# Attention folded into a feed-forward layer: products of one head each, grouped by parity and packed eight to the array, with decode clamps on GpSimd and a new early order

## The chip, the cores and the metric

The kernel runs on one core of a Trainium2 chip (trn2). The metric is the device time of one launch in microseconds (us). Before the change three runs gave 717.12, 719.28 and 719.66 us; the median is 719.28. All data start and end in the chip's main memory (DRAM). A core has five engines with their own instruction streams: TensorE (PE), VectorE (DVE), ScalarE (ACT), GpSimd (POOL) and SyncE (SP); nearly all transfers are issued by SP.

## The reference, cut to what matters

```python
B, H, S, Ns, D = 8, 8, 512, 32, 64           # x [B,H,S,D], state [B,H,Ns,D]
scores  = x @ state.T / sqrt(D)              # per batch and head, 512 x 32
xread   = softmax(scores) @ state            # 512 x 64
scores2 = state @ x.T / sqrt(D)              # the transpose of the same scores
sread   = softmax(scores2) @ x               # 32 x 64
t = concatenate([xread, sread])              # 544 tokens a batch, 8 heads x 64 = 512 features
out = (maximum(t @ w_in, 0) ** 2) @ w_out    # w_in 512 x 2048, w_out 2048 x 512
```

There are 8 x 544 = 4352 tokens. Inputs x and state are float32; w_in and w_out arrive as 64-bit floats, which the kernel reads as pairs of 32-bit words and turns into float32 on the chip ("decode").

## The kernel before, in words

**The fold.** xread @ w_in is softmax(scores) @ (state @ w_in), head by head. So the kernel never forms xread. It makes, for each batch b, the matrix W2[b] = state_h @ w_in_h for the eight heads h: 8 x 32 = 256 rows and 2048 columns. The first layer for the 512 x-tokens of a batch is then a product over K = 256 (two groups of 128 rows, called g) of the softmax and W2[b]. The 256 sread tokens of all batches are "block 8" and use w_in itself (K = 512).

**The two large steps.** The 2048 hidden columns are 16 pieces `fc` of 128, two to an `hb` of 256. Wide products are exact to about float32: each operand is split into a high part and a remainder (`_hi`, `_lo`, type float32r) and three products are added (`mm3`, line 325): hi x hi, hi x lo, lo x hi. `hidden(blk, fc)` makes 128 x 512 hidden values in PSUM (tile `ph`, 6 matmuls of 512 columns), ACT and DVE square them and split them into `g_hi` and `g_lo`. `accumulate(blk, fc)` adds their products with w_out into four PSUM tiles `acc` (12 matmuls of 512 columns). Blocks 0 and 1 are done in two halves of eight `fc`; their partial results wait in DRAM.

**W2 before** has three ways. `direct_w2` (batches 0 and 1) multiplies in float32: `by_head` (line 349) uses the array in parts of 64 rows and 32 columns, with heads 4g..4g+3 at the four column strips and the row half given by the head's parity; one call of `direct_w2` makes 8 such matmuls, 256 columns each. `quad_w2` (lines 705 and 706; tile `qps`, batches 2 to 5) stacks four batches' states of a head to 128 rows and uses whole-array float32r products. `paired_w2` (tile `w2ps`, from `mm3`, batches 6 and 7) uses block-diagonal states and three products. Results of all but hb 0 to 3 of batches 0 and 1 go to DRAM and come back through `load_w2`.

**Scores before.** For batches 0 and 1 `scores` calls `by_head` in float32, 4 matmuls for each g. For the others x is transposed by DVE, split (lines 302 and 303) and multiplied by block-diagonal states `bd_hi` and `bd_lo` (tile `st`, 6 matmuls of 512 columns for each g). `sread` (line 515, tile `pr`) makes 16 small matmuls for each g. `transposes` (line 500) prepares it. `prep` makes the transposed x.

**Decode.** A piece of 128 x 512 weights takes one operation on ACT (line 337, absolute value) and four on DVE: a clamp (338), a shift (339) and two that merge bits (340, 341). There are 16 pieces of w_in (`decode_wi`) and 16 of w_out (`prep_wo`).

**What sets the order.** PLAN is a long string of steps ("hidden.2.4 accumulate.2.2 ..."); they are walked in that order, and a step's needs must stand ahead of it. SECOND is a table that sends single operations to the second of two engines. On top of that the framework's scheduler, which simulates a timeline, may move instructions past one another on each engine; instructions marked `keep_in_program_order` stay. PSUM has eight banks in three pools: four for `acc`, two for `ph`, two for everything else (`ps_b`, tag `psb`: W2, scores of batches 1 to 7, transposes, sread). SBUF buffers are shared by tags, so a tile waits until the last user of its buffer is done.

Of the kernel before, what the change touches and what calls it, by code (L numbers as in the profile page):

```python
# [18 lines left out]

# [4 lines left out]

PLAN = """
    load_raw.0 load_wo.1 zero_bd.1.1 load_direct ident neg_ident decode_wi.0 load_raw.1 decode_wi.1 start.0
        prep.0.0 load.0.1 prep.0.1 zero_bd.0.1 load_raw.3 start.1 load_raw.2 load_wo.4 states scores.0.0
        direct_w2.0 decode_wi.3 decode_wi.2 load_wo.0 direct_w2.1 load_wo.2 transposed_scores.0.0 exp_s.0.0
        transposes.0.0 softmax.0.0 sread.0.0 prep_wo.0 load_wo.3 direct_w2.2 load_wo.7 scores.0.1
        transposed_scores.0.1 exp_s.0.1 prep_wo.1 transposes.0.1 prep.1.0 sread.0.1 prep_wo.3 scores.1.0  # L30
        transposed_scores.1.0 load_raw.5 load_raw.4 load.1.1 direct_w2.3 softmax.0.1
    hidden.0.0 accumulate.0.0 prep.1.1 prep_wo.2
    hidden.0.1 decode_wi.4 decode_wi.5 load_wo.5 direct_w2.4 scores.1.1 load_raw.6 decode_wi.6 prep_wo.4
        load_raw.7
    hidden.0.2 direct_w2.6 exp_s.1.0 direct_w2.5 transposed_scores.1.1
# [11 lines left out]
    hidden.1.4 decode_wi.14 qw2.0.13 accumulate.1.2 decode_wi.15 accumulate.1.4 qw2.0.14
    hidden.1.1 accumulate.1.1
    hidden.1.5 accumulate.1.5
    hidden.0.8  # L50
    hidden.1.6 prep_wo.13 accumulate.1.3 qw2.0.15 load_wo.14 load_quad.1 prep_wo.14 load_w2.0.5 accumulate.1.6
    hidden.1.7 load_wo.15
    hidden.0.9 load_w2.0.7 start.2 prep.2.0 sread.1.1 load_w2.0.6 qload.1.4 scores.2.0 prep_wo.15
        accumulate.0.8 prep_quad.1 qload.1.0 qprep.1.0 qprep.1.4 accumulate.0.9
    hidden.0.10
# [21 lines left out]
    hidden.2.5 load_w2.2.3 scores.3.0 qw2.1.10
    hidden.2.4 qload.1.13 qw2.1.11 qprep.1.13 accumulate.2.2
    hidden.2.6 load_w2.2.4 accumulate.2.1 qload.1.14 load_w2.2.5 load.3.1 prep.3.1 qprep.1.12 qw2.1.12
    hidden.2.7 qw2.1.13 accumulate.2.4 accumulate.2.6  # L80
    hidden.2.8 qprep.1.14 qload.1.15 qprep.1.15 load_w2.3.0 qw2.1.14 accumulate.2.7 transposed_scores.3.0
        load_n.3.0
    hidden.2.10 exp_s.3.0
    hidden.2.9 transposes.3.0 load_w2.2.6
    hidden.2.12 scores.3.1 accumulate.2.3 transposed_scores.3.1 qw2.1.15 load_w2.2.7 load_quad.2
        accumulate.2.8 sread.3.0 accumulate.2.10 softmax.3.0 softmax.3.1
    hidden.2.11 split_wi.0 split_wi.1 accumulate.2.9 load_w2.3.1
# [129 lines left out]
def tile_attn_moe(  # L217
# [791 lines left out]
```

## Time and profile before

| what | value |
|---|---|
| runs | 717.12, 719.28, 719.66 us; median 719.28 |
| span of the profiled execution | 715.2 us, which is 4.1 below the median of the runs |
| PE, DVE, ACT, POOL busy | 676.1, 409.6, 377.1, 118.4 us |
| instructions counted | PE 3797, DVE 734, ACT 725, POOL 118 |
| moved by DMA | 113.57 MB, mean 159 GB/s |

The profile is of one execution. A row of a group gives a line of the kernel, the engine, the operation, "output<-inputs" with tile names without their numbers, the shape, a count, the busy time, the mean time of one, and the idle time of the engine just ahead of these instructions with what ended it. A row of the timeline gives the start, the length and the same names. A float32 product in parts of the array appears as two records, so x16 in such a row is eight matmuls of the program. Matmuls overlap: the length of one is a latency, and its price is the distance to the start of the next.

### The profile page before, as it was taken

To read this page: it belongs to the slowest core of one execution; us is meant where nothing else is said; L and a number is where in the kernel's file an instruction comes from. 1 tells how busy PE (TensorE), PEld (TensorE's weight loads), DVE (VectorE), ACT (ScalarE), POOL (GpSimd) and SP (SyncE) were. 2 spreads that over 40 slices of the span, in tenths; PEclk is the share of its full clock that TensorE was granted. 3 is DMA by queue.
4 is the path that set the end of the run, shared out by engine and by line. 5 is a ranking of instruction groups with operands and counts; after the bars stand their busy time and mean duration, and the time that the engine had idled before them with its cause. 6 is when DMAs were issued, how large, how long until landed. Compare 5 with 4: busy or idle time off the path is not lost.

```text
span 715.2 us, 10699 instructions
## 1 busy us (share of the span) xinstructions
PE 676.1 (95%) x3797; PEld 542.4 (76%) x3797; DVE 409.6 (57%) x734; ACT 377.1 (53%) x725; POOL 118.4 (17%) x118
## 2 busy tenths in 40 slices
PE   4497889999999999999999999999999999999997
PEld 2265566677888788888878888888888888888886
DVE  4999889599665587574444564466347222322233
ACT  3576664577665466555535565556455443333323
POOL 1321222044101214123220230012011000000000
PEclk9699999999999999999999999999999999999999
DMA  9936576645764753664426244752576334444402
GB/s 240 261 95 216 176 250 194 233 148 175 238 196 136 203 177 107 207 216 151 147 76 212 98 148 134 248 165 87 163 206 185 81 83 131 127 118 119 118 1 88
DMA packets 93797, 113.57 MB, mean 159 GB/s; under 512 B 24752, under 2 KB 63920, under 8 KB 93744
## 3 DMA queue, kind: packets, MB, share of 16 engines
q1 hardware_dynamic: 93600, 112.76, 51.5%
q8 instruction: 30, 0.49, 0.3%
q14 instruction: 23, 0.19, 0.1%
q10 hardware_dynamic: 144, 0.13, 0.1%
HBM read 70.39 MB, written 42.47 MB: 158 GB/s over the span
## 4 chain that ended last, share of the span: by engine, by line
PE 79%; DVE 7%; issue 4%; DMA 4%; ACT 2%; SPq 1%; POOL 1%; DVEq 0%; ACTq 0%; POOLq 0%
PE acc L325 45%; PE ph L325 25%; PE st L325 2%; PE w2ps L325 2%; PE pr L515 1%; DMA xp<-in_x_dram 1%; DMA part_d<-po 1%; PE w2ps L349 1%; PE qps L705 1%; PE qps L706 1%; PE pt L500 1%; DVE deco L341 1%; DVE g_lo L766 1%; DVE deco L340 1%; DMA std<-in_state_dram 1%
## 5 line engine op out<-in xcount | busy, mean ns | idle before, releaser
L325 PE MATMUL acc<-wo,g_hi 128*128 128x512 f32 x1086 | 312.9, 392 | 4.4 <-ACT g_hi L761 4.3
L325 PEld LDWEIGHTS acc<-wo,g_hi 128*128 128x128 f32 x1086 | 200.8, 188 | 49.0 <-ACT g_hi L761 6.4
L325 PE MATMUL acc<-wo,g_lo 128*128 128x512 f32 x543 | 187.4, 393 | 1.0 <-ACT g_lo L764 0.5
L325 PE MATMUL ph<-k_hi,w 128*128 128x512 f32 x512 | 182.9, 399 | 3.5 <-DVE g_lo L766 3.1
L766 DVE TENSOR_TENSOR g_lo<-ph,g_hi 128x512 fp32r<-128x512 f32 (+1 forms) x139 | 90.6, 654 | 119.7 <-ACT g_hi L761 115.4
L325 PEld LDWEIGHTS acc<-wo,g_lo 128*128 128x128 f32 x543 | 100.6, 188 | 22.6 <-DVE g_lo L766 1.5
L325 PEld LDWEIGHTS ph<-k_hi,w 128*128 128x128 f32 x512 | 97.2, 191 | 26.5 <-DVE g_lo L766 4.2
L761 ACT CAST g_hi<-ph 128x512 fp32r<-128x512 f32 (+1 forms) x144 | 81.0, 564 | 50.3 <-DVE ph L760 35.3
L325 PE MATMUL ph<-k_lo,w 128*128 128x512 f32 x256 | 101.1, 395 | 0.1
L760 DVE SCALAR_TENSOR_TENSOR ph<-ph,r 128x512 f32<-128x512 f32 (+1 forms) x78 | 51.1, 655 | 70.5 <-ACT r L759 70.4
L759 ACT ACTIVATE r<-ph 128x512 f32<-128x512 f32 (+1 forms) x78 | 44.3, 568 | 83.0 <-PE ph L325 82.9
L755 ACT ACTIVATE ph<-ph 128x512 f32<-128x512 f32 (+1 forms) x66 | 37.2, 566 | 66.6 <-PE ph L325 66.3
L325 PEld LDWEIGHTS ph<-k_lo,w 128*128 128x128 f32 x256 | 48.7, 190 | 9.8 <-POOL k_lo L303 0.9
L303 POOL TENSOR_TENSOR w<-w_f,w 128x512 fp32r<-128x512 f32 x19 | 25.2, 1324 | 120.0 <-ACT w L302 111.3
L756 ACT ACTIVATE ph<-ph 128x512 f32<-128x512 f32 (+1 forms) x66 | 37.7, 571 | 1.2
L349 PE MATMUL w2ps<-dec,sT 64*32 64x256 f32 x256 | 18.4, 412 | 18.3 <-DVE dec L341 10.6
L302 ACT CAST w<-w_f 128x512 fp32r<-128x512 f32 x40 | 24.7, 616 | 17.1 <-DMA w_f<-w_d 11.9
L391 DVE STREAM_TRANSPOSE xT<-xp 128x512 f32<-128x512 f32 x24 | 16.9, 706 | 24.1 <-DMA xp<-in_x_dram 22.4
L349 PEld LDWEIGHTS w2ps<-dec,sT 64*32 64x32 f32 x256 | 7.4, 112 | 26.0 <-issue 11.4
L303 POOL TENSOR_TENSOR x_lo<-xT,x_hi 128x512 fp32r<-128x512 f32 x10 | 13.3, 1328 | 80.9 <-ACT x_hi L302 58.4
L325 PE MATMUL ph<-sr_hi,s 128*128 128x256 f32 x128 | 25.5, 282 | 0.0
L302 ACT CAST x_hi<-xT 128x512 fp32r<-128x512 f32 x24 | 14.9, 620 | 14.2 <-DVE xT L391 12.4
(124 smaller groups left out, 783.0 us busy)
## 6 DMA issues: line engine op xcount, KB each, us to landing
wi_raw<-in_moe_w_in_dram SPq DMA_DIRECT2D x16, 512.0 KB, 4.4
wo_raw<-in_moe_w_out_dram SPq DMA_DIRECT2D x16, 512.0 KB, 5.4
w_d<-qo SPq DMA_DIRECT2D x64, 128.0 KB, 2.1
w_f<-w_d SPq DMA_DIRECT2D x32, 256.0 KB, 3.4
win_d<-wi SPq DMA_DIRECT2D x16, 512.0 KB, 3.2
w<-w2a_d SPq DMA_DIRECT2D x32, 256.0 KB, 4.1
s<-win_d SPq DMA_DIRECT2D x128, 64.0 KB, 2.0
out_dram<-o SPq DMA_DIRECT2D x31, 256.0 KB, 3.8
```

Of the source, the lines that this page charges most:

```text
L302: nc.scalar.copy(hi, src)
L303: pick(key, nc.gpsimd, nc.vector).tensor_sub(lo, src, hi.bitcast(F32))
L325: m = nc.tensor.matmul(ps, l, r, start=first and i == 0, stop=last and i == len(seq) - 1, skip_group_check=skip)
L340: nc.vector.scalar_tensor_tensor(v, high, 0xC0000000, v, ALU.bitwise_and, ALU.bitwise_or)
L349: nc.tensor.matmul(out[v], sT[0][q, NC * b + 2 * g + h // 2], x[q], start=start, stop=stop, tile_position=(64 * (h % 2), 32 * h), **kw,)
L391: nc.vector.transpose(xT.rearrange("p (k j s) -> p k j s", k=KC, j=4), self.xp[g].rearrange("p (j k d) -> p k j d", j=4, k=KC)[..., 32 * e ...
L755: nc.scalar.activation(ph, ph, AF.Relu)
L756: nc.scalar.activation(ph, ph, AF.Square)
L759: nc.scalar.activation(r, ph, AF.Relu)
L760: nc.vector.scalar_tensor_tensor(ph, ph, 0.0, r, ALU.max, ALU.mult)
L761: nc.scalar.copy(ghi, ph)
L766: nc.vector.tensor_sub(glo, ph, ghi.bitcast(F32))
```

## The change: what it does

- **Heads by parity.** `by_head` now makes eight products of 64 rows and 32 columns: head 2c + g at column strip c and row half g. The two halves write to two different PSUM banks (`out[g]`). The states of all batches lie in `sT` in this layout; `load_states` and `states` fill it for batches 0 and 1 and then for 2 to 7. Block-diagonal states, `prep_state`, `zero_bd` and the split of x are gone.
- **Scores** of all batches, both groups at once, are one call of `by_head` in float32 (8 matmuls of 512 columns).
- **W2** of all batches is made by `two_w2`, for two batches and one hb at a time: 16 matmuls of 256 columns into two `psb` tiles, that is, both buffers of that pool. There are 8 hb x 4 pairs = 32 such calls, from `direct_w2` (0 and 1), `later_w2` (2 and 3, 4 and 5) and `last_w2` (6 and 7). `quad_*`, `paired_*` and `split_wi` are gone. Float32 w_in is read back from DRAM by `load_wf`.
- **sread** is one step for both groups (32 matmuls into one PSUM tile).
- **Decode**: the clamp is on POOL for 13 of the 16 pieces of w_in (all but 0, 2 and 3) and for 14 of w_out (all but 5 and 10), 27 of 32 in all.
- **Loads**: x of batches 2 to 7 comes in 8 transfers for each g instead of 4; the weights of block 8 come as float32 and are split on the chip (`load_wi`), where before their two parts were read back.
- **Order**: PLAN's early part does `direct_w2` for hb 0 and 1, scores and softmax of batch 0, sread of batch 0 and one piece of w_out ahead of the first hidden step; steps of batch 1 and more pieces of w_out, which stood there before, come behind it. From there on accumulate follows hidden at a distance of two steps almost throughout.

```diff
-    def by_head(out, b, g, h, x, start, stop, **kw):
-        q, v = slice(64 * (h % 2), 64 * (h % 2) + 64), slice(32 * h, 32 * h + 32)
-        nc.tensor.matmul(
-            out[v], sT[0][q, NC * b + 2 * g + h // 2], x[q],
-            start=start, stop=stop, tile_position=(64 * (h % 2), 32 * h), **kw,
-        )
+    def by_head(out, b, x, start, stop, **kw):
+        for c in range(NC):
+            for g in range(G):
+                q, v = slice(64 * g, 64 * g + 64), slice(32 * c, 32 * c + 32)
+                nc.tensor.matmul(
+                    out[g][v], sT[q, NC * b + c], x(c)[q],
+                    start=start, stop=stop, tile_position=(64 * g, 32 * c), **kw,
+                )
...
+    def two_w2(hb, b0, last):
+        w = (wf.pop(hb) if last else wf[hb]).bitcast(F32)
+        ps = [ps_b.tile([P, 2, HB], F32, tag="psb", name=f"w2ps{hb}_{b0}_{g}") for g in range(G)]
+        for b in range(2):
+            by_head([t[:, b] for t in ps], b0 + b, lambda c: w[:, c], b == 0, True, skip_group_check=True)
+        return ps
...
+    def keep_w2(hb, b0, ps):
+        for g in range(G):
+            o = p2.tile([P, 2, HB], F32, tag="o", name=f"w2o{hb}_{b0}_{g}", bufs=4)
+            evac(f"w2_out.{hb}.{b0}.{g}", o, ps[g])
+            nc.sync.dma_start(w2_d[hb][b0 : b0 + 2, :, g].rearrange("b p f -> p b f"), o)
+
+    def later_w2(hb, b0):
+        keep_w2(hb, b0, two_w2(hb, b0, b0 == 4))
...
-                mm3(
-                    st,
-                    [((bhi[:, g * E + e], blo[:, g * E + e]), (x[0][:, e], x[1][:, e])) for e in range(E)],
-                )
+            for g in range(G):
+                self.st[g] = pool.tile([P, S], F32, tag=tag, name=f"st{b}_{g}")
+            by_head(self.st, b, lambda c: self.x[c // 2][:, c % 2], True, True)
...
-        nc.vector.tensor_scalar(vf, vf, F64_HI_MIN, F64_HI_MAX, ALU.max, ALU.min)
+        eng = pick(key, nc.vector, nc.gpsimd)
+        eng.tensor_scalar(vf, vf, F64_HI_MIN, F64_HI_MAX, ALU.max, ALU.min)
...
-                nc.tensor.matmul(ps[:, h2], s4[0][:, h], t[:, c, h2], start=True, stop=False)
-                nc.tensor.matmul(ps[:, h2], s4[1][:, h], t[:, c, h2], start=False, stop=True)
...
-            mm3(ps[:, c], [((s4[0][:, k], s4[1][:, k]), (w[:, c, 0], w[:, c, 1]))])
...
-                        nc.sync.dma_start(t[32 * h : 32 * h + 32, 2 * i : 2 * i + 2].bitcast(F32), rows[:, :, j])
+            split(hi[:, q], lo[:, q], f[:, q], f"w_in_lo.{hb}.{i}")
...
-    hidden.4.8 scores.5.1 qw2.2.6 load_w2.4.6 accumulate.4.6 transposed_scores.5.1
+    hidden.4.8 softmax.5.0 load_n.5.0 load_n.5.1 accumulate.4.6
```

**Where the order changes: PE, W2 of batches 2 to 5.** Before, in the stretch of hidden block 0, `fc` 12, the eight matmuls of one `quad_w2` call stand as one piece between accumulate and hidden (`qps` is the PSUM tile, `tt` the split weights, `s_hi` and `s_lo` the split states):

```order
L325 MATMUL acc_8_3_1476<-wo_985,g_lo_10_1529 128x512
L705 MATMUL qps_0_0_1616<-tt_1499,s_hi 128x256
L706 MATMUL qps_0_0_1616<-tt_1499,s_lo 128x256
L705 MATMUL qps_0_1_1625<-tt_1499,s_hi 128x256
L706 MATMUL qps_0_1_1625<-tt_1499,s_lo 128x256
L705 MATMUL qps_0_0_1616<-tt_1499,s_hi 128x256
L706 MATMUL qps_0_0_1616<-tt_1499,s_lo 128x256
L705 MATMUL qps_0_1_1625<-tt_1499,s_hi 128x256
L706 MATMUL qps_0_1_1625<-tt_1499,s_lo 128x256
L325 MATMUL ph_12_1658<-k_hi_149,w_0_6_1450 128x512
```

Now, at the same place of the program, eight matmuls of the pair 2 and 3 and eight of the pair 4 and 5 stand in the middle of an accumulate (a tile `w2ps_2_1` belongs to the pair that begins with batch 2, row half 1):

```order
L291 MATMUL acc_8_0_2085<-wo_1212,g_hi_10_1992 128x512 x2
L291 MATMUL acc_8_0_2085<-wo_1212,g_lo_10_1993 128x512
L291 MATMUL acc_8_1_2086<-wo_1212,g_hi_10_1992 128x512 x2
L317 MATMUL w2ps_2_1_2038<-wf_1_1841,sT 32x256 x8
L317 MATMUL w2ps_4_0_2061<-wf_1_1841,sT 32x256 x8
L291 MATMUL acc_8_1_2086<-wo_1212,g_lo_10_1993 128x512
L291 MATMUL acc_8_2_2087<-wo_1212,g_hi_10_1992 128x512 x2
```

The whole-array products of `quad_w2` are gone, and the products in parts of the array stand with all eight of one row half in a row.

**PE, W2 of batches 6 and 7.** Before, one `paired_w2` call stands as one piece between hidden block 3, `fc` 9, and accumulate:

```order
L325 MATMUL ph_9_3451<-k_hi_2262,w_3_4_3195 128x512
L325 MATMUL w2ps_2_3598<-wi_3342,s_hi 128x256 x2
L325 MATMUL w2ps_2_3598<-wi_3342,s_lo 128x256
L325 MATMUL w2ps_2_3598<-wi_3342,s_hi 128x256 x2
L325 MATMUL w2ps_2_3598<-wi_3342,s_lo 128x256
L325 MATMUL acc_0_0_3049<-wo_760,g_hi_6_3386 128x512 x2
```

Now the first call of `last_w2`, in block 2 and 3, stands like this, with eight more of its matmuls some 25 rows further on:

```order
L291 MATMUL acc_0_3_2508<-wo_1639,g_lo_15_3049 128x512
L317 MATMUL w2ps_6_0_3238<-wf_2_2863,sT 32x256
L317 MATMUL w2ps_6_1_3239<-wf_2_2863,sT 32x256
L291 MATMUL ph_2_3152<-k_hi_2308,w_3_1_3055 128x512
L291 MATMUL ph_2_3152<-k_lo_2309,w_3_1_3055 128x512
L291 MATMUL ph_2_3152<-k_hi_2308,w_3_1_3055 128x512 x2
L291 MATMUL ph_2_3152<-k_lo_2309,w_3_1_3055 128x512
L291 MATMUL ph_2_3152<-k_hi_2308,w_3_1_3055 128x512
L317 MATMUL w2ps_6_0_3238<-wf_2_2863,sT 32x256
L317 MATMUL w2ps_6_1_3239<-wf_2_2863,sT 32x256
L317 MATMUL w2ps_6_0_3238<-wf_2_2863,sT 32x256
L317 MATMUL w2ps_6_1_3239<-wf_2_2863,sT 32x256
```

The 16 matmuls of one call are spread over several places between hidden and accumulate.

**DVE, the first operations.** Before, both clamps (L338) of the first two pieces of w_in stand on DVE (`sT` is the transpose of the states):

```order
L338 TENSOR_SCALAR dec_133<-dec_133 128x512
L339 TENSOR_SCALAR dec_133<-dec_133 128x512
L340 SCALAR_TENSOR_TENSOR dec_133<-wi_raw_117,dec_133 128x512
L541 STREAM_TRANSPOSE sT<-std_122 128x256
L341 SCALAR_TENSOR_TENSOR dec_133<-wi_raw_117,dec_133 128x512
L338 TENSOR_SCALAR dec_142<-dec_142 128x512
L339 TENSOR_SCALAR dec_142<-dec_142 128x512
L340 SCALAR_TENSOR_TENSOR dec_142<-wi_raw_140,dec_142 128x512
```

Now the second piece has no clamp there; it is the L305 of POOL:

```order
L305 TENSOR_SCALAR wf_128<-wf_128 128x512
L478 STREAM_TRANSPOSE sT<-std_103 128x256
L306 TENSOR_SCALAR wf_128<-wf_128 128x512
L307 SCALAR_TENSOR_TENSOR wf_128<-wi_raw_101,wf_128 128x512
L308 SCALAR_TENSOR_TENSOR wf_128<-wi_raw_101,wf_128 128x512
L306 TENSOR_SCALAR wf_128<-wf_128 128x512
L307 SCALAR_TENSOR_TENSOR wf_128<-wi_raw_114,wf_128 128x512
L308 SCALAR_TENSOR_TENSOR wf_128<-wi_raw_114,wf_128 128x512
```

The clamp of the second piece has moved from DVE to POOL, and the transposed states have moved up by two places.

More of the change, by code (lines that the diff above doesn't have):

```diff
@@ L47 @@
[L47 to L55, printed above, removed]
@@ L77 @@
[L77 to L86, printed above, removed]
@@ new lines @@
+    hidden.2.12 accumulate.2.10
+    hidden.2.13 sread.3 load_w2.3.0 accumulate.2.11
+    hidden.2.14 accumulate.2.12
+    hidden.2.15 load_w2.3.1 accumulate.2.13
+    hidden.3.0 start.4 accumulate.2.14
+    hidden.3.1 load_w2.3.2 accumulate.2.15
+    hidden.3.2 load.4.1 prep.4.0 accumulate.3.0
+    hidden.3.3 load_w2.3.3 accumulate.3.1
+    hidden.3.4 last_w2.2 load_wf.2.3 accumulate.3.2
+    hidden.3.5 prep.4.1 load_w2.3.4 accumulate.3.3
+    hidden.3.6 accumulate.3.4
+    hidden.3.7 scores.4 transposed_scores.4.0 exp_s.4.0 transposed_scores.4.1 exp_s.4.1 load_w2.3.5
+        accumulate.3.5
@@ new lines @@
+    hidden.3.8 softmax.4.0 load_n.4.0 load_n.4.1 accumulate.3.6
+    hidden.3.9 load_w2.3.6 accumulate.3.7
+    hidden.3.10 softmax.4.1 last_w2.3 load_wf.2.4 accumulate.3.8
+    hidden.3.11 transposes.4.0 transposes.4.1 load_w2.3.7 accumulate.3.9
+    hidden.3.12 accumulate.3.10
+    hidden.3.13 sread.4 load_w2.4.0 accumulate.3.11
+    hidden.3.14 accumulate.3.12
+    hidden.3.15 load_w2.4.1 accumulate.3.13
+    hidden.4.0 start.5 accumulate.3.14
+    hidden.4.1 load_w2.4.2 accumulate.3.15
+    hidden.4.2 load.5.1 prep.5.0 accumulate.4.0
@@ new lines @@
+    hidden.4.12 accumulate.4.10
+    hidden.4.13 sread.5 load_w2.5.0 accumulate.4.11
+    hidden.4.14 accumulate.4.12
+    hidden.4.15 load_w2.5.1 accumulate.4.13
+    hidden.5.0 start.6 accumulate.4.14
+    hidden.5.1 load_w2.5.2 accumulate.4.15
+    hidden.5.2 load.6.1 prep.6.0 accumulate.5.0
+    hidden.5.3 load_w2.5.3 accumulate.5.1
+    hidden.5.4 last_w2.6 load_wf.2.7 accumulate.5.2
+    hidden.5.5 prep.6.1 load_w2.5.4 accumulate.5.3
+    hidden.5.6 accumulate.5.4
+    hidden.5.7 scores.6 transposed_scores.6.0 exp_s.6.0 transposed_scores.6.1 exp_s.6.1 load_w2.5.5
+        accumulate.5.5
@@ new lines @@
+    hidden.5.8 softmax.6.0 load_n.6.0 load_n.6.1 accumulate.5.6
+    hidden.5.9 load_w2.5.6 accumulate.5.7
+    hidden.5.10 softmax.6.1 last_w2.7 accumulate.5.8
+    hidden.5.11 transposes.6.0 transposes.6.1 load_w2.5.7 accumulate.5.9
+    hidden.5.12 accumulate.5.10
+    hidden.5.13 sread.6 load_w2.6.0 accumulate.5.11
+    hidden.5.14 accumulate.5.12
+    hidden.5.15 load_w2.6.1 accumulate.5.13
+    hidden.6.0 start.7 accumulate.5.14
+    hidden.6.1 load_w2.6.2 accumulate.5.15
+    hidden.6.2 load.7.1 prep.7.0 accumulate.6.0
@@ L153 @@
+    hidden.6.12 load_wi.0 accumulate.6.10
     hidden.6.13 accumulate.6.11
@@ new lines, in direct_w2 @@
+        first = (
+            w2_tile(0, hb),
+            cp.tile([P, G, 2, HB], F32R, tag=f"wo{NFC - DH + hb}", name=f"w2_1_{hb}"),
+        )
+        for b in range(2):
+            t = first[b]
+            for g in range(G):
+                nc.scalar.copy(t[:, g, 0], ps[g][:, b])
+                if f"w2_pe.{hb}.{b}.{g}" in second:
+                    minus_hi(ps[g][:, b], t[:, g, 0])
+                    nc.scalar.copy(t[:, g, 1], ps[g][:, b])
+                else:
+                    nc.vector.tensor_sub(t[:, g, 1], ps[g][:, b], t[:, g, 0].bitcast(F32))
+            weights[b, hb] = hi_lo(t)
@@ L911, in tile_attn_moe @@
                 "transposes": [key("exp_s", b, g), "ident"],
-                "sread": [key("load_n", b, g)] * (not early) + [key("transposes", b, g)],
             }
@@ L957, in tile_attn_moe @@
         step(key("load_part", b), load_part, b, after=[key("accumulate", b, HF - 1)])
-    step("split_sread", split_sread, after=[key("sread", b, g) for b in range(B) for g in range(G)])
+    step("split_sread", split_sread, after=[key("sread", b) for b in range(B)])
     for blk in range(B + 1):
```

607 lines of the change are left out of this document (216 added, 391 removed).

## The prediction, on record before the result

> **What bounds the kernel now.** I read the page first, then busy time by stage, then the groups of TensorE (PE) and VectorE (DVE), then single stretches of the timeline. The page's first line says that PE is busy for nearly the whole span:
>
> ```profile
> PE 676.1 (95%) x3797; PEld 542.4 (76%) x3797; DVE 409.6 (57%) x734; ACT 377.1 (53%) x725; POOL 118.4 (17%) x118
> ```
>
> A mean hides stages, so the second view is the busy time of stretches that I chose (stretch, length, then PE, weight loads, DVE, ACT, POOL, granted clock, DMA share, GB/s):
>
> ```profile
> 0.00:36.00 36.00, 17.17 (x128) 8.55 (x129) 25.99 (x52) 16.05 (x30) 9.55 (x15) 0.81 0.93 252
> 36.00:144.00 108.00, 95.63 (x650) 66.84 (x649) 91.16 (x175) 68.26 (x138) 22.60 (x22) 0.98 0.58 192
> ...
> 180.00:700.00 520.00, 518.72 (x2818) 430.83 (x2817) 253.76 (x442) 260.63 (x497) 70.68 (x67) 1.00 0.48 146
> ```
>
> From 180 to 700 us PE idles 1.3 us in 520, while DVE, ACT and POOL are each half idle or more. There, only what PE itself executes counts; work taken off the other engines or the DMA engines is worth nothing. From 36 to 144 us PE idles 12.4 us and DVE works 91 of 108: that stage is shared between PE and the decode of the weights. In the first 36 us PE idles 18.8.
>
> The groups of PE that the change removes or rewrites (output<-inputs, count, then busy total, mean ns, idle before and what ended it):
>
> ```profile
> L349 PE MATMUL w2ps<-dec,sT 64*32 64x256 f32 x256 | 18.4, 412 | 18.3 <-DVE dec L341 10.6 <-DVE r L461 6.9 <-ACT ph L755 0.8
> ...
> L705 PE MATMUL qps<-tt,s_hi 128*128 128x256 f32 x64 | 16.3, 283 | 0.0
> L706 PE MATMUL qps<-tt,s_lo 128*128 128x256 f32 x64 | 16.3, 282 | 0.0
> L325 PE MATMUL w2ps<-wi,s_hi 128*128 128x256 f32 x64 | 12.6, 284 | 0.0
> ...
> L325 PE MATMUL st<-x_hi,bd_hi 128*128 128x512 f32 x24 | 9.6, 400 | 0.3 <-ACT x_hi L302 0.3
> L325 PE MATMUL st<-x_lo,bd_hi 128*128 128x512 f32 x24 | 9.5, 395 | 0.4 <-POOL x_lo L303 0.4
> L325 PE MATMUL st<-x_hi,bd_lo 128*128 128x512 f32 x24 | 9.4, 390 | 0.0
> L325 PE MATMUL w2ps<-wi,s_lo 128*128 128x256 f32 x32 | 9.0, 282 | 0.0
> ```
>
> A mean of 0.28 to 0.40 us is a matmul's latency, not its price, because matmuls overlap. The price is the distance from start to start, in a stretch where PE never waits (start, us, engine, line, tile):
>
> ```profile
> 299.14 0.39 PE L325 MATMUL ph<-k_hi,w 128*128 128x512 f32 x1
> 299.37 0.40 PE L325 MATMUL w2ps<-wi,s_hi 128*128 128x256 f32 x2
> 299.60 0.28 PE L325 MATMUL w2ps<-wi,s_lo 128*128 128x256 f32 x1
> ```
>
> 512 columns take 0.23 us (0.227 over a long run of such starts), and two products of 256 columns take the same, 0.12 each.
>
> **What the main stage loses.** All L705, L706, paired and st products lie after 144 us. 128 qps at 0.12 are 15.4 us, 96 paired at 0.12 are 11.5, 72 st at 0.227 are 16.3: 43.2 us off PE.
>
> **What the main stage gains.** The same results now come from float32 products in parts of the array (64x32). Before has that form in its early stage, among 128x128 products:
>
> ```profile
> 128.17 0.61 PE L325 MATMUL acc<-wo,g_hi 128*128 128x512 f32 x2
> 128.72 1.07 PE L349 MATMUL w2ps<-dec,sT 64*32 64x256 f32 x16
> 129.72 0.50 PE L325 MATMUL acc<-wo,g_lo 128*128 128x512 f32 x1
> 130.05 0.62 PE L325 MATMUL acc<-wo,g_hi 128*128 128x512 f32 x2
> ```
>
> ```profile
> 103.51 0.39 PE L325 MATMUL ph<-k_hi,w 128*128 128x512 f32 x1
> 103.83 1.93 PE L349 MATMUL w2ps<-dec,sT 64*32 64x256 f32 x32
> 105.69 0.50 PE L325 MATMUL ph<-k_hi,w 128*128 128x512 f32 x1
> 106.03 0.40 PE L325 MATMUL ph<-k_lo,w 128*128 128x512 f32 x1
> ```
>
> Each float32 product leaves two records. Eight products (16 records), four side by side, cost 130.05 - 128.17 less three 512-column products: 1.20 us. Sixteen (32 records) cost 106.03 - 103.51 less two: 2.07. The difference, 0.87, is four more passes of the array, so a pass of 256 columns is 0.217 us and what is left, 1.20 - 4x0.217 = 0.33, is paid once for every visit: going from whole-array products to parts of it and back. A short visit shows that this part does not shrink with the work:
>
> ```profile
> 365.78 0.39 PE L325 MATMUL ph<-k_hi,w 128*128 128x512 f32 x1
> 366.10 0.31 PE L515 MATMUL pr<-xn,eT 128*32 128x64 f32 x6
> 366.34 0.50 PE L325 MATMUL acc<-wo,g_hi 128*128 128x512 f32 x1
> ```
>
> Three small products take 0.33 us beyond the 0.227 before the next one starts, and that one is late itself, as above (0.33 instead of 0.227): 0.43 for almost no columns.
>
> With eight side by side, one W2 product for two batches (16 matmuls) would again be 1.20. Undisturbed, 24 of them (28.8) and six scores (0.33 + 4x0.217 = 1.20 each, 7.2) would put back 36.0 of the 43.2: a gain of 7.2. The Trainium skill ("TensorEngine Tiling (Array Packing)", Tiling Modes) gives 64x32 eight independent tiles, and by that alone the sum of this paragraph would be the result. The same page says under Key Properties that a change of tiling mode drains the engine, which speaks against this change; the 0.33 per visit agrees with it.
>
> But the order in which the changed program stands on PE breaks them up. From blocks 0 and 1 on to the end I count 52 visits, not 30: the later W2 products and the scores are cut into two to five pieces, with hidden and accumulate products between. And in eight W2 pairs all eight matmuls of one row half stand before the eight of the other; since matmuls in the trace start in their order, a pass cannot take from both halves except where they meet: six passes instead of four. In all 200 passes of 256 columns (148 W2, 52 scores). 52x0.33 + 200x0.217 = 60.6 us put in for 43.2 taken out: +17.4. sread in one visit for a batch instead of two saves 7 visits of 0.33 there, -2.3. **Main stage: +15.1 us.**
>
> Bounds: if the halves ran free of one another, 180 passes, 56.2 us, +10.7 with sread. If only four products run side by side as in before's rows (the two halves never together), I count about 231 passes, +21.8. The new eight are bounded by these; I take the order's count because the four of before already share the array across both halves. A wait for the two PSUM buffers, both of which a W2 pair now takes, I cost at nothing: before uses both in turn without a break, and the 1.3 us idle of the main stage bounds what that costs there; if the cover of interleaved products were gone, it would be one eviction per pair.
>
> **The early stage.** The decode's clamp leaves DVE in 27 of 32 cases. The group of those for w_out before 140 us (output<-input, count, busy, mean ns, idle before):
>
> ```profile
> L338 DVE TENSOR_SCALAR deco<-deco 128x512 f32<-128x512 f32 x14 | 5.9, 422 | 12.0 <-ACT deco L337 11.7
> ```
>
> 27 x 0.42 = 11.3 us off DVE. With prep_quad goes one stall near the start as well (rows of the timeline from 21 to 30 us; SPq is SP's queue of DMA issues):
>
> ```profile
> 21.05 0.65 DVE L341 SCALAR_TENSOR_TENSOR dec<-wi_raw,dec 128x512 uint32<-128x512 uint32 x1
> ...
> 24.61 1.23 DVE L673 STREAM_TRANSPOSE sqT<-sq 128x1024 f32<-128x1024 f32 x1
> ...
> 27.09 3.45 POOL L303 TENSOR_TENSOR s_lo<-sqT,s_hi 128x512 fp32r<-128x512 f32 x2 [2.68 <-ACT s_hi L302]
> 27.36 1.79 DVE L341 SCALAR_TENSOR_TENSOR dec<-wi_raw,dec 128x512 uint32<-128x512 uint32 x1
> 29.15 1.42 DVE L474 TENSOR_SCALAR s<-s 128x16 f32<-128x16 f32 x1
> ...
> 29.57 0.43 SPq L733 DMA_DIRECT2D wo_raw<-in_moe_w_out_dram  x1
> ```
>
> A POOL operation on one tile of 512 columns, from the page:
>
> ```profile
> L303 POOL TENSOR_TENSOR w<-w_f,w 128x512 fp32r<-128x512 f32 x19 | 25.2, 1324 | 120.0 <-ACT w L302 111.3
> ```
>
> sqT (1.23) goes. While POOL runs, the same L341 takes 1.79 instead of 0.65, and an L474 on 16 columns takes 1.42, twice a whole L341 on 512: some 1.14 + 1.3 = 2.4 lost in 3.45 us of POOL, 0.7 of its time. So a clamp on POOL is not free for DVE. The trace has none; its nearest row is the 1.32 us of a POOL subtraction. Bounds for what one clamp takes from DVE: nothing, to 0.7 of 1.32, 0.93. I take 0.33, nearer to nothing, because a clamp reads one tensor and the subtraction two: 27 x 0.33 = 9. (The Trainium skill, "GPSIMD Engine Reference", Specifications, tells of contention with DVE's instructions of two SBUF inputs; the L341 row agrees.) DVE is relieved by 11.3 + 1.2 + 2.4 - 9 = 6, and I take as much off the span, since PE's wait ahead of W2 ends mostly on the decode (10.6 of 18.3 on L341). Bounds: -15 (all relief, no stall) to +10 (27 x 0.93 = 25 of stalls). PE's own tiled work there falls too, from 18 visits and 84 passes to 15 and 62 (24.2 to 18.4), beside the same waits, so I do not add it. The 16 issues that load batch 2 now stand on SP ahead of the raw weights 6 and 7: at the 0.43 us of the last row but one, 16 x 0.43 = 7 us of SP's queue. Those weights are wanted for the fourth W2 product, dozens of microseconds on, so I cost it at nothing; without that cover it is up to 7, inside the bounds.
>
> Other edits at nothing: the late weights' splits on ACT, DVE and POOL, the smaller loads and stores, the missing splits of x all lie beside a full PE; the cover ends only if one of them grows past half the stage.
>
> **Sum.** +15.1 - 6 = +9. The profiled execution spans 715.2, 4.1 below the median of 719.28, so I add the difference to the median: 728.
>
> **Rivals.**
> *(a) The halves run free of one another*: 180 passes, +10.7 - 6 = +4.7: 724. For it: four tiles start together already across halves. Against: starts are in order in every row I read. The Trainium skill ("TensorE: Matmul & The Clock Gate", Part 3, The mechanism) has matmuls strictly first in, first out in start and end; by that the passes stay at six and this rival falls.
> *(b) Faster: the start gives more than the main stage takes.* Mechanism: decode on DVE is the pace of 0 to 144 us, and both a lighter DVE and early products in a better order let PE close its idle time. At most it closes the 12.4 us idle of 36 to 144, saves the 5.8 us of tiled work and a little of the 18.8 at the start; about 20 of it gives 715.2 - 20 + 15.1 + 4.1 = 714. It decides from 18.7 us (15.1 + 3.6) on. For: 10.6 us of waits end on the decode. Against: loads fill 0.93 of the first stage, which nothing here shortens, and POOL's stalls.
> *(c) Fewer side by side, so the change does not do what it says*: row halves share something and only four run at once: +21.8 - 6 = +16, 735; with POOL's full stalls 740 or more.
>
> **How the numbers follow.** Forecast 0.46 (728), (a) 0.14 (724), (b) 0.19 (714), (c) 0.21 (735 to 741). About 0.5%, 3.6 us, is what a measurement can tell from no change: 715.7 to 722.9 is "same". Faster gets (b) but for its weak end and a little of (a): 0.21. Same gets the lower parts of (a) and of the forecast: 0.14. Slower 0.65. The range takes the forecast, (a), most of (c) and the nearer half of (b): 715 to 740.
>
> **What would show it.** Right: between 180 us and the end PE stays busy without idle, and its stretch is some 15 us longer for the same blocks; every visit of L317 costs 0.33 plus 0.217 a pass; runs with one half first cost about 1.63, not 1.20; the first 144 us of work end some 6 us earlier. Wrong: passes of eight that cost twice 0.217 (case c), visits of 16 matmuls at 1.20 whatever their order (case a), PE idle in the early stage below 5 us and blocks 0 and 1 done 20 us sooner (case b), or new PE idle for w2ps buffers in the main stage.

## The result, and the profile after

The changed kernel takes 725.57 us (median of 4 runs, 724.65 to 726.98), the kernel before 718.2 on the same chips (4 runs). The ratio is 1.0121, with a 95% interval of 1.0084 to 1.0157: slower by about 1.2%. The profiled execution spans 722.8 us, 7.6 more than before. Runs of later sections stood on other chips, where the kernel before took 715.0 to 716.8; they are compared by their ratio to it.

The page of the changed kernel, and its stretches, with the columns as in the prediction:

```profile
PE 684.7 (95%) x4365; PEld 516.4 (71%) x4365; DVE 382.0 (53%) x659; ACT 333.0 (46%) x638; POOL 137.3 (19%) x95
```

```profile
0.00:36.00 36.00, 16.03 (x170) 8.61 (x171) 24.11 (x50) 13.89 (x29) 14.00 (x15) 0.82 0.92 242
36.00:144.00 108.00, 95.50 (x688) 66.31 (x688) 89.91 (x146) 62.32 (x125) 59.39 (x32) 0.93 0.70 221
144.00:180.00 36.00, 35.18 (x261) 24.95 (x268) 27.74 (x52) 22.09 (x42) 16.74 (x11) 1.00 0.57 186
180.00:700.00 520.00, 520.00 (x3179) 401.47 (x3164) 233.26 (x401) 227.91 (x431) 47.17 (x38) 1.00 0.39 114
```

From 180 to 700 us PE is busy without a gap, and DVE, ACT and the DMA engines have lost work there (DVE 254 to 233, ACT 261 to 228, DMA share 0.48 to 0.39): that relief was worth nothing. From 36 to 144 us PE is as busy as before, DVE a little less, and POOL 59.4 us in place of 22.6; the granted clock was lower there, 0.93 in place of 0.98.

The groups that took the place of qps, paired w2ps and st:

```profile
L317 PE MATMUL w2ps<-wf,sT 64*32 64x256 f32 x1024 | 51.7, 393 | 2.9 <-DVE wf L308 1.6 <-ACT w L537 1.2
...
L317 PE MATMUL st<-xT,sT 64*32 64x512 f32 x128 | 20.5, 601 | 1.6 <-ACT xT L279 1.4 <-ACT w2o L279 0.2
```

What they cost is seen in the timeline. Here PE works through half of one W2 call of batches 6 and 7, in three pieces:

```profile
385.79 0.39 PE L291 MATMUL acc<-wo,g_lo 128*128 128x512 f32 x1
386.10 0.62 PE L317 MATMUL w2ps<-wf,sT 64*32 64x256 f32 x4
386.66 0.50 PE L291 MATMUL ph<-k_hi,w 128*128 128x512 f32 x1
386.99 0.39 PE L291 MATMUL ph<-k_lo,w 128*128 128x512 f32 x1
387.22 0.63 PE L291 MATMUL ph<-k_hi,w 128*128 128x512 f32 x2
387.69 0.39 PE L291 MATMUL ph<-k_lo,w 128*128 128x512 f32 x1
387.91 0.40 PE L291 MATMUL ph<-k_hi,w 128*128 128x512 f32 x1
388.24 0.64 PE L317 MATMUL w2ps<-wf,sT 64*32 64x256 f32 x8
388.81 0.73 PE L291 MATMUL acc<-wo,g_hi 128*128 128x512 f32 x2
389.37 0.40 PE L291 MATMUL acc<-wo,g_lo 128*128 128x512 f32 x1
389.70 0.62 PE L317 MATMUL w2ps<-wf,sT 64*32 64x256 f32 x4
390.25 0.73 PE L291 MATMUL acc<-wo,g_hi 128*128 128x512 f32 x2
```

The first piece, two products, takes 386.66 - 385.79 - 0.227 = 0.64 us and leaves the next start 0.10 late (386.99 - 386.66 is 0.33): 0.75. The second, four products, costs 0.78, the third, two, 0.76. A whole call of 16 costs 1.23 in this trace. So these eight products took 2.3 us, and the call's other eight 0.8 later.

**PE's account.** From the starts of all PE instructions I charged each whole-array product its distance (0.2275 us for 512 columns, 0.12 for 256, 0.109 for 128), counted products in parts of the array, with what is late beside them (up to 0.12 on a side), as visits, and called the rest idle. In us, with the time of the last start. Hidden and accumulate, 569.0, are the same in all rows, and so, within 1 us or so, are some 21 for the time ahead of the first product, the transposes and other small products:

| kernel | visits | whole-array W2 and scores | idle | last start |
|---|---|---|---|---|
| before | 41.0 | 43.3 | 36.6 | 710.96 |
| changed | 92.0 | 0 | 35.6 | 717.73 |

51.0 put in, 43.3 taken out, 1.0 less idle: 6.7, and the last starts differ by 6.8. After that the two kernels differ by 0.8 at their ends.

Each row is of one execution, and how much is called visits and how much idle depends by about 1 us on the 0.12. Idle also holds what whole-array products took beyond their price while the granted clock was 0.50. In the changed kernel that lasted longer; first a stretch of the kernel before, then of the changed one:

```profile
23.00:36.00 13.00, 6.22 (x27) 3.53 (x28) 12.83 (x26) 6.40 (x11) 5.78 (x4) 0.50 0.90 276
```

```profile
23.50:43.50 20.00, 12.62 (x118) 8.44 (x119) 19.97 (x39) 11.09 (x25) 17.81 (x11) 0.50 0.93 229
```

With a shorter stretch near 80 us the clock was at half for some 17 us before and 27 us now, and the products that started then took some 3 and some 5.5 us beyond their price.

### The profile page after: what moved, and what is told of

It reads as the page before. It is cut to its first block, busy times and chain, and to the rows that moved or that the text cites. A ratio compares the mean times of both kernels' runs of the same rounds, so it can differ in the third digit from the quotient of the medians.

```text
span 722.8 us, 11420 instructions
## 1 busy us (share of the span) xinstructions
PE 684.7 (95%) x4365; PEld 516.4 (71%) x4365; DVE 382.0 (53%) x659; ACT 333.0 (46%) x638; POOL 137.3 (19%) x95
## 4 chain that ended last, share of the span: by engine, by line
PE 79%; DVE 6%; DMA 4%; SPq 3%; POOL 3%; issue 2%; ACT 2%; DVEq 0%; ACTq 0%; POOLq 0%
PE acc L291 46%; PE ph L291 24%; PE w2ps L317 5%; DMA wo_raw<-in_moe_w_out_dram 2%; PE st L317 2%; SPq L340 2%; DMA wi_raw<-in_moe_w_in_dram 1%; POOL dec L305 1%; PE pr L453 1%; DVE wf L308 1%; DVE wf L307 1%; POOL wf L305 1%; SPq L427 1%; PE pt L438 1%; DVE dec L308 1%
## 5 line engine op out<-in xcount | busy, mean ns | idle before, releaser
L291 PE MATMUL acc<-wo,g_hi 128*128 128x512 f32 x1086 | 326.9, 396 | 1.2 <-DVE po L277 1.1
L291 PE MATMUL acc<-wo,g_lo 128*128 128x512 f32 x543 | 197.1, 393 | 0.0
L291 PEld LDWEIGHTS ph<-k_hi,w 128*128 128x128 f32 x512 | 97.1, 190 | 36.6 <-issue 5.0
L317 PE MATMUL w2ps<-wf,sT 64*32 64x256 f32 x1024 | 51.7, 393 | 2.9 <-DVE wf L308 1.6
L317 PEld LDWEIGHTS w2ps<-wf,sT 64*32 64x32 f32 x1024 | 20.7, 107 | 25.5 <-issue 12.2
L269 POOL TENSOR_TENSOR s<-sf,s 128x512 fp32r<-128x512 f32 x8 | 10.3, 1291 | 134.8 <-ACT s L268 97.3
L305 POOL TENSOR_SCALAR dec<-dec 128x512 f32<-128x512 f32 x14 | 31.3, 2246 | 17.9 <-ACT dec L304 17.9
L305 POOL TENSOR_SCALAR wf<-wf 128x512 f32<-128x512 f32 x13 | 26.5, 2044 | 34.7 <-ACT wf L304 34.7
L352 DVE STREAM_TRANSPOSE xT<-xp 128x512 f32<-128x512 f32 x24 | 24.4, 1083 | 15.1 <-DMA xp<-in_x_dram 7.7
```

The lines of the kernel that those rows point to most:

```text
L269: pick(key, nc.gpsimd, nc.vector).tensor_sub(lo, src, hi.bitcast(F32))
L291: m = nc.tensor.matmul(ps, l, r, start=first and i == 0, stop=last and i == len(seq) - 1, skip_group_check=skip)
L305: eng.tensor_scalar(vf, vf, F64_HI_MIN, F64_HI_MAX, ALU.max, ALU.min)
L317: nc.tensor.matmul(out[g][v], sT[q, NC * b + c], x(c)[q], start=start, stop=stop, tile_position=(64 * g, 32 * c), **kw,)
L352: nc.vector.transpose(xT[:, c].rearrange("p (k s j) -> p k j s", k=KC, j=4), self.xp[g][:, c].rearrange("p (j k d) -> p k j d", j=4, k=KC),)
```

## The experiments

**Whole calls by a critical section** (e1_unbroken), and the same with the loads of e3 (e4_unbroken_xp_late). The edit, for scores as well:

```diff
-        for b in range(2):
-            by_head([t[:, b] for t in ps], b0 + b, lambda c: w[:, c], b == 0, True, skip_group_check=True)
+        with tc.tile_critical():
+            for b in range(2):
+                by_head([t[:, b] for t in ps], b0 + b, lambda c: w[:, c], b == 0, True, skip_group_check=True)
```

> The changed kernel with each call of scores and of a W2 pair kept in one piece on PE, so 40 visits to the 64x32 form instead of 67, all with the two row halves alternating. Theory A (PE is full after 180 us, and a broken call pays 0.33 us again for each further piece, and passes of columns with some of the eight places empty): the 52 later visits cost 58.5 us in the changed kernel's trace; 30 whole ones at 1.23 are 36.8, so some 21 us go: 704 us, 700 to 708, which is also faster than the kernel before by some 14. Rival B (the pieces fill places where PE would wait, since a whole call needs both PSUM buffers of its pool at once): PE idle after 180 us takes the place of the pieces and the gain is under 8 us: 718 or more.

> Both edits, whole calls and the loads of x kept in place. If the two act in different stages, they add: theory A of both gives about 700 us, 696 to 706. If the early stage is set by the decode alone, the same as with whole calls only.

Measured: 795.98 us, ratio 1.1128 (1.1101 to 1.1155), and 807.72, 1.1292 (1.1267 to 1.1318). Neither theory: the section did keep the calls whole, but brought waits of its own. In the waits of PE of e1 (line, what it waited for: us in total, times, longest) W2 now waits on things that it doesn't use:

```profile
PE w2ps L317 <- issue: 11.6, 9, 5.8
PE w2ps L317 <- DMA w_d<-w2o: 11.3, 4, 4.8
...
PE w2ps L317 <- POOL sp L415: 4.6, 1, 4.6
PE w2ps L317 <- DVE dec L306: 3.9, 1, 3.9
```

These two runs say nothing on the price of a piece; the pinned kernels below ask again.

**Clamps back on DVE** (e2_clamp_dve): two lines of SECOND are taken out.

```diff
-    decode_wi: 1 4 5 6 7 8 9 10 11 12 13 14 15
-    decode_wo: 0 1 2 3 4 6 7 8 9 11 12 13 14 15
```

> The changed kernel with all 32 clamps back on DVE. Theory A (what DVE is relieved of comes back as stalls and as a longer decode chain, so the clamps are worth about nothing): within 3 us of the changed kernel, 722 to 728. Rival B (the relief of 6 us off the span that the prediction put down): 730 or more. Rival C (the clamp of 2.1 us on POOL is itself what delays the early stage): 721 or less.

Measured: 723.33 us, ratio 1.0102 (1.0074 to 1.0129), against 1.0121 for the changed kernel: no difference beyond the intervals, so theory A as a sum. Its account is less simple: idle falls from 35.6 to 29.1 and visits grow from 92.0 to 95.5, since the scheduler, given other early operations, cuts the early calls in other places.

**Loads of x kept in place** (e3_xp_late):

```diff
-                        nc.sync.dma_start(
+                        m = nc.sync.dma_start(
                             xp[o : o + 32, c].rearrange("p (t d) -> p t d", d=32),
...
+                        tc.keep_in_program_order(m)
```

In the changed kernel the 16 issues hold SP's queue for 13 us:

```profile
32.88 13.40 SPq L340 DMA_DIRECT2D xp<-in_x_dram  x16
```

> The changed kernel with the 8 + 8 loads of x of a later batch kept in SP's queue where the program has them, so that those of batch 2 no longer stand ahead of the raw weights 6 and 7. Theory A (the 12 us that these issues hold SP's queue from 33 to 46 us are on the chain of the early stage): 2 to 6 us faster than the changed kernel, 720 to 724. Rival B (hidden, since PE and DVE have other work there): within 2 us, 724 to 727. Rival C (x of batch 2 now comes late): slower.

Measured: 727.86 us, ratio 1.02 (1.015 to 1.025). Theory A fails in the sum. The accumulate and hidden products reach their 241st start at 126.2 us in place of 129.7; by the last start the kernel is 1.7 behind, with visits at 94.9 in place of 92.0. That the queue cost those 3.5 us is not shown: raw weight 6, which stood behind the 16 issues, is issued at nearly the same time in the changed kernel and here, and weight 7 as well (51.35 and 51.15 us):

```profile
48.49 0.39 SPq L489 DMA_DIRECT2D wi_raw<-in_moe_w_in_dram  x1
```

```profile
48.28 0.38 SPq L490 DMA_DIRECT2D wi_raw<-in_moe_w_in_dram  x1
```

The order of the early operations moved too, so what gained the 3.5 us stays open. So does why the medians differ by more than the profiled spans (724.5 and 722.8); one of the four runs took 734 us.

**PE pinned to the order of the program** (e5_pinned). From `later_w2.0.2` on every matmul and transpose is kept behind the one before it, and PLAN has one W2 call for one hidden step:

```diff
+            m = nc.tensor.matmul(*a, **kw)
+            return tc.keep_in_program_order(m) if pe.on else m
...
+        pe.on = pe.on or k == "later_w2.0.2"
...
-    hidden.1.6 later_w2.0.2 later_w2.0.4 load_wf.1.1 load_w2.0.5 accumulate.1.4
-    hidden.1.7 prep_wo.12 load_wo.14 accumulate.1.5
...
+    hidden.1.6 load_w2.0.5 later_w2.0.2 load_wf.1.1 accumulate.1.4
+    hidden.1.7 prep_wo.12 load_wo.14 later_w2.0.4 accumulate.1.5
```

> The critical section of the first run carried waits of its own, so whole calls again, by another way: from the first W2 product for batches 2 and 3 on, every product on PE stays in the order of the program, and the steps that make W2 for batches 2 to 5 are spread, one call for one hidden step. Main stage: 29 visits instead of 52, all with the halves alternating. Theory A (PE is full, pieces cost 0.33 us each and half-empty passes): 58.5 us of visits become about 36, so 22 off the changed kernel's ratio of 1.012: 0.98 of the kernel before, 0.975 to 0.988, faster than both kernels. Rival B (the scheduler's pieces hide waits for the two PSUM buffers and for g): PE idle after 180 us grows by 10 us or more, and the ratio stays above 0.995.

Measured: 722.86 us, ratio 1.0106 (1.0067 to 1.0145). Rival B in the sum, but the account shows both: visits 74.2 in place of 92.0, so 17.8 us were saved, and idle 50.0 in place of 35.6, so 14.4 were lost. Most of the loss lies ahead of 320 us; the waits of PE from 144 to 320 us there:

```profile
PE w2ps L254 <- DVE w2o L277: 5.3, 3, 3.1
PE w2ps L254 <- ACT e L389: 4.7, 1, 4.7
PE acc L254 <- DVE o L664: 2.1, 1, 2.1
```

A W2 call waits for both buffers of its pool: for the eviction (w2o) of the call before it, or for scores to be read (e). In the changed kernel the same stretch has 0.9 us of waits:

```profile
PE acc L291 <- DVE po L277: 0.7, 2, 0.4
PE st L317 <- ACT w2o L279: 0.2, 1, 0.2
```

There the pieces did cover waits, as rival B has it. Most of the rest of the loss is the clock: it was at half for some 41 us here, in place of 27, and whole-array products overran their price then by some 8.5 us in place of 5.5. From the 901st hidden or accumulate product to the last the pinned kernel takes 387.4 us, the changed one 399.6: there theory A holds alone.

**The price of a visit alone** (e7_pinned_two_pieces): a W2 call of batches 2 to 7 makes its first batch, and the second, with what follows it, after the next three accumulate products.

```diff
+        piece(0)
...
+        pending.append(lambda: (piece(1), then(ps)))
...
+            while pending:
+                pending.pop(0)()
```

> As the pinned kernel, with each of the 24 later W2 calls cut into two pieces of eight products (both halves, so two full passes each), with three accumulate products between: 24 more visits and not one more pass. Theory A (a visit has a fixed price of 0.33 us on a full PE): 24 x 0.33 = 7.9 us slower than the pinned kernel, 7 to 9. Rival B (the price lies in the half-empty passes alone, or is hidden): under 3 us.

Measured: 729.64 us, ratio 1.0191 (1.0174 to 1.0209); by the profiled spans 9.0 us slower than the pinned kernel (727.9 and 718.9), by the medians 6.8. Visits grow by 8.8 us, 0.37 for each of the 24 new ones, and idle by -0.3. Theory A.

**Row half by row half** (e8_pinned_half_by_half):

```diff
-        for b in range(2):
-            by_head([t[:, b] for t in ps], b0 + b, lambda c: w[:, c], b == 0, True, skip_group_check=True)
+        for g in range(G):
+            for b in range(2):
+                by_head([t[:, b] for t in ps], b0 + b, lambda c: w[:, c], b == 0, True, (g,), skip_group_check=True)
```

> As the pinned kernel, with all eight products of one row half ahead of the eight of the other in each W2 call. The prediction's step (starts in order, so six passes in place of four): 2 x 0.217 = 0.43 for each of 24 calls, 10 us slower than the pinned kernel. Rival (a) of the prediction (the halves run free of one another; visits of that order took 1.25 to 1.33 in the changed kernel where alternating ones took 1.23): 0.03 to 0.1 each, under 3 us.

Measured: 729.49 us, ratio 1.0187 (1.0168 to 1.0206). The sum looks like the prediction's step, and the trace says otherwise: by the last start this kernel is 8.5 us behind the pinned one, and 6.6 of them are there by the 241st product (137.1 and 130.5 us), in the stretch that isn't pinned, where the scheduler dealt the calls anew. From the 901st product on this kernel takes 387.4 us, the pinned one 387.4. One visit of it, eight products of one half ahead of eight of the other:

```profile
139.62 0.39 PE L254 MATMUL ph<-k_hi,w 128*128 128x512 f32 x1
139.94 1.12 PE L254 MATMUL w2ps<-wf,sT 64*32 64x256 f32 x32
140.99 0.73 PE L254 MATMUL acc<-wo,g_hi 128*128 128x512 f32 x2
```

140.99 - 139.62 is 1.37 us; six passes would make it 1.75. With alternating halves it is 1.34, in e9 below. The halves run free of one another.

**Pinned clamps** (e6_pinned_clamp_dve): e5 with the edit of e2.

> As the pinned kernel, with all clamps back on DVE. With the order of PE fixed behind the early stage, the early stage's difference reaches the end. Theory A (the clamps on POOL bring about nothing, since what DVE is relieved of comes back as stalls): within 3 us of the pinned kernel. Rival B (each clamp of 2.1 us on POOL lengthens the decode's chain; with it on DVE PE idled 29.1 us in place of 35.6): 4 to 7 us faster than the pinned kernel. Rival C (the prediction's relief): 6 us slower.

Measured: 719.0 us (8 runs), ratio 1.004 (1.0023 to 1.0057): by the medians 4 to 5 us less than the pinned kernel, as rival B has it. The traces do not bear that out: the last starts differ by 1.1 us (idle 45.0 in place of 50.0, visits 78.0 in place of 74.2), and the pinned kernel's four runs fall into two pairs, 720.4 and 720.7, 725.0 and 725.7, of which the lower is the one profiled. So between rival B and theory A it stays open.

**Pinned late** (e9_late_pinned): PLAN as in the changed kernel, and as the only edit, beside e5's `pe`,

```diff
+        pe.on = pe.on or k == "hidden.2.0"
```

> The changed kernel, with PE in the order of the program only from the first hidden step of block 2 on (about 235 us); ahead of that its order on PE is the changed kernel's, row for row. From there on 16 visits of whole calls take the place of 35 that cost 35.9 us in the changed kernel's trace, and 5 of sread the place of 9. Theory A (pieces and half-empty passes are what the change pays; the pinned kernel lost its gain to waits before 315 us, where W2 for batches 2 to 5 follows call on call and each needs both PSUM buffers): 16 x 1.23 = 20, and 6 in place of 7.8 for sread: 17 us less PE work, less up to 4 of new idle; ratio 0.992, 0.988 to 0.997, faster than both kernels. Rival B (waits for g and the two buffers come with any fixed order): idle grows as it did in the first pinned kernel, ratio 1.005 or more.

Measured: 711.14 us (6 runs), ratio 0.9921 (0.9903 to 0.9939): faster than both kernels, by 0.8% and, against 1.0121, by 2.0%. Visits 71.8, idle 42.8, last start 704.44: 20.2 of PE work less than the changed kernel for 7.2 of idle more. The call that stands in three pieces and more above is here one visit, 1.34 from start to start:

```profile
393.25 0.39 PE L267 MATMUL ph<-k_hi,w 128*128 128x512 f32 x1
393.57 1.09 PE L267 MATMUL w2ps<-wf,sT 64*32 64x256 f32 x32
394.59 0.73 PE L267 MATMUL acc<-wo,g_hi 128*128 128x512 f32 x2
```

**The same with clamps on DVE** (e10_late_pinned_clamp_dve, with the edit of e2), **and with no clamp** (e11_no_clamp):

```diff
-        eng.tensor_scalar(vf, vf, F64_HI_MIN, F64_HI_MAX, ALU.max, ALU.min)
```

> As the late pinned kernel, with all clamps back on DVE. The other pair with this difference gave 4 us less (clamps back alone) and 4 us less (pinned). Theory A (the clamps on POOL are no gain and cost some 4 us of PE idle in the early stage): 2 to 6 us faster than the late pinned kernel, ratio 0.987. Rival B (an accident of the scheduler's order): within 2 us of it. Rival C (the prediction's relief): slower than it.

> As the late pinned kernel, with no clamp on any engine: the 32 operations are left out, so 64-bit weights outside the range of float32 would be decoded wrongly. It bounds what the decode's clamp can be worth. Theory A (decode on DVE sets the pace of the first 144 us): 13 us less DVE work against clamps on DVE bring 5 to 10 us against that kernel. Rival (the loads and the order set the pace there): within 3 us.

Measured: 710.87 us, ratio 0.9925 (0.9906 to 0.9943), so no difference from e9: rival B. Of the three pairs two show nothing and one shows 4 to 5 us by the medians and 1.1 in the trace, so where the clamp runs has no effect of its own that these runs can tell from the scheduler's dealing. Without any clamp 706.61 us, ratio 0.9863 (0.984 to 0.9885): 4 us against either, between the two theories. All 32 clamps together are worth about that much here, with the dealing of the early calls in it.

**A control** (e12_before_pinned): the kernel before, with e5's `pe` and

```diff
+        pe.on = pe.on or k == "hidden.4.0"
```

> A control: the kernel before with PE in the order of the program from the first hidden step of block 4 on (a fixed order from block 2 on isn't possible in it). Its visits there are whole already (sread at 0.79 us each). Theory A (the late pinned kernel is faster because whole calls take the place of pieces): nothing to gain, within 2 us of the kernel before, ratio 0.997 to 1.003. Rival (the fixed order of hidden and accumulate is itself what gains): 5 us or more faster, ratio 0.993 or less.

Measured: 715.72 us (12 runs), ratio 0.9985 (0.997 to 1.0). From block 4 on a fixed order as such gains some 1 us; theory A. It does not reach back to block 2, where e9's order begins. But from the 901st product on e9 takes 387.4 us in place of the changed kernel's 399.6, and its account there has visits of 17.4 in place of 31.7 and idle of 2.4 in place of 0.2: the fewer visits are enough for the 12.2 us.

The accounts of the runs of which the text speaks, as above:

| kernel | visits | idle | last start |
|---|---|---|---|
| clamps on DVE (e2) | 95.5 | 29.1 | 713.80 |
| loads of x late (e3) | 94.9 | 34.1 | 719.39 |
| pinned (e5) | 74.2 | 50.0 | 713.76 |
| pinned, clamps on DVE (e6) | 78.0 | 45.0 | 712.65 |
| pinned, two pieces (e7) | 83.0 | 49.7 | 722.81 |
| pinned, half by half (e8) | 80.5 | 52.4 | 722.27 |
| pinned late (e9) | 71.8 | 42.8 | 704.44 |
| pinned late, clamps on DVE (e10) | 75.4 | 40.7 | 706.21 |
| pinned late, no clamp (e11) | 73.9 | 36.5 | 699.11 |

## Why the prediction was right, point by point

The direction, the main cause and the size held: slower, because the order on PE breaks the products up. The terms of the sum were less good than the sum. The forecast was +9, as 15.1 - 6; the medians on the same chips differ by 7.4, the profiled spans by 7.6, as 12.6 in the main stage, -5.8 for the rest, and 0.8 at the ends.

- **What the main stage loses**: 43.2 us forecast, 43.3 in the account.
- **What it gains**: 60.6 forecast for 52 visits. The 52 visits add up to 58.5 us. The fixed price held: 0.33 forecast, 0.37 in e7. The step that failed is "a pass cannot take from both halves except where they meet: six passes instead of four". Visits in that order take 1.25 to 1.33 us, not 1.63, and the order of e8 costs next to nothing where PE is pinned: this was rival (a), 56.2 us, and the remainder up to 58.5 is some 1.2 to 1.4 us of waits inside two visits, the few hundredths by which those visits are longer, and the fixed price a little above 0.33. The rule of the Trainium skill by which I let that rival fall ("TensorE: Matmul & The Clock Gate", Part 3, The mechanism: matmuls start and end in strict order) did not carry over to two row halves as I read it. The eight independent tiles that the Trainium skill gives ("TensorEngine Tiling (Array Packing)", Tiling Modes) did, with 1.23 us for a whole call against 1.20 estimated.
- **sread**: -2.3 forecast. Ten visits (8.8 us) stand for 17 (11.4): -2.6.
- **The early stage**: -6 forecast. The last starts differ by 6.8, of which 58.5 - 43.3 - 2.6 = 12.6 are the main stage, so -5.8 are left for the rest. That is the forecast number by another road, and that the numbers agree is luck. I put it down to DVE's relief, "since PE's wait ahead of W2 ends mostly on the decode (10.6 of 18.3 on L341)". But 8.9 of the 10.6 are the wait of the kernel's first product, counted from the start of the span, and the changed kernel's first product waits as long for a load of x. First the kernel before, then the changed one:

```profile
8.92 1.93 PE L349 MATMUL w2ps<-dec,sT 64*32 64x256 f32 x16 [8.92 <-DVE dec L341]
```

```profile
8.98 0.66 PE L361 MATMUL px<-ident,xn 128*128 128x128 f32 x2 [8.98 <-DMA xn<-in_x_dram]
```

  Behind that, W2 waited 1.7 us on the last merge before and 1.6 now. DVE's busy time in the first 144 us fell by 3.1 us (25.99 + 91.16 to 24.11 + 89.91), not by 6. And the sign that I named, the first 144 us of work done some 6 us earlier, did not come: the 241st hidden or accumulate product starts at 129.7 us, before at 125.5, with some 5 us more idle ahead of it. The changed kernel has less idle only behind that, some 6 us up to the 901st product; there, before the change, hidden products waited 3.1 us for g_lo from DVE, and now they don't. Which edit moved the idle is not shown; e2, with the clamps back on DVE, has 6.5 us less of it. I also left PE's own tiled work out ("beside the same waits"). The account has 1.0 less idle in all, 2.2 to 2.4 less if the waits just named are left aside; the other 3.4 to 3.6 are that work. Both steps failed, and they cancel.
- **The stall of a clamp**: 0.33 forecast. The shift and the last merge got longer where POOL ran. First the kernel before, then the changed one (DVE groups before 140 us):

```profile
L341 DVE SCALAR_TENSOR_TENSOR deco<-wo_raw,deco 128x512 uint32<-128x512 uint32 x13 | 9.9, 772 | 0.0
...
L339 DVE TENSOR_SCALAR dec<-dec 128x512 uint32<-128x512 uint32 x16 | 7.6, 475 | 0.2
```

```profile
L308 DVE SCALAR_TENSOR_TENSOR dec<-wo_raw,dec 128x512 uint32<-128x512 uint32 x13 | 12.9, 1001 | 0.0
...
L306 DVE TENSOR_SCALAR wf<-wf 128x512 uint32<-128x512 uint32 x16 | 10.3, 644 | 3.3 <-POOL wf L305 3.3
```

  Over the decode's three operations that stay on DVE the groups grow from 59.0 to 66.3 us, 7.3 or 0.27 for each of 27 clamps. Against e2, where the clamps are on DVE and POOL has less to do than in either, the same groups take 55.5, so it is 10.8 us or 0.40 for each. So of the 11.3 us taken off DVE two thirds came back as stalls by the first comparison, and nearly all by the second. That POOL is the cause is seen in the changed kernel's single operations: those with POOL at work for more than 0.3 of their time took 774 ns in the shift and 852 and 982 in the two merges on average, the others 416, 683 and 685. DVE's chain got longer besides, since a clamp on POOL takes 2.0 to 2.2 us where I had 1.32 as the nearest row:

```profile
L305 POOL TENSOR_SCALAR dec<-dec 128x512 f32<-128x512 f32 x14 | 31.3, 2246 | 17.9 <-ACT dec L304 17.9
L305 POOL TENSOR_SCALAR wf<-wf 128x512 f32<-128x512 f32 x13 | 26.5, 2044 | 34.7 <-ACT wf L304 34.7
```

- **The loads of x on SP**, costed at nothing: their 16 issues took 13.4 us of the queue, not 7, and yet no run shows a cost, since raw weights 6 and 7 were issued only 0.2 us earlier without them (e3).
- **The PSUM buffers**, costed at nothing: right for the changed kernel, and by the reason given, the interleaved pieces are the cover. e5 took the cover away and paid 12 us in the waits shown there, 10 of them ahead of W2.
- **Rival (b)** needed 18.7 us of the early stage; it gave 5.8. **Rival (c)** falls: eight run side by side.

What the change gave away is shown by e9: with whole calls where nothing has to be covered, the same design is 0.8% faster than the kernel before. What the best order ahead of 235 us would be is open; the one other order that was tried there, e5's, lost.

## What to carry to other kernels

Where PE is full, cost products in parts of the array by the visit, and read the number of visits from the order that the scheduler makes, not from the source: a piece of two products costs 0.75 us, a whole call of sixteen 1.23. Keep such calls whole where PE never waits, and let them be cut only where the pieces cover a wait. When an edit moves the scheduler's dealing, split the difference of two runs into PE work and idle before believing the sum: several edits here (clamps back on DVE, both pinned pairs) moved the two in opposite directions, by 3 to 18 us. And before a wait is costed by its total, find its longest part in the timeline: here that was the time ahead of the first product, and it was as long after the change.

## What the runs showed of the hardware that was not expected

A score piece of a single 512-column product costs as much as all eight: visits of 2 records took 1.17 us in the changed kernel, visits of 16 took 1.22 in e9. And the two row halves of the array need not be fed in turn: eight products of one half ahead of eight of the other took 1.25 to 1.33 us where alternating ones took 1.23.
